# Earlier row loads, later filter weights and a third inverse-output buffer in a fused spectral filter and gated linear kernel

## The chip, the cores and the metric

The kernel runs on one core of a Trainium2 chip. The metric is the time of one execution on the device in microseconds (us). All runs that this text compares were classed as fast. Four of them had a granted clock of 0.992, the others 1.00: two timed runs of u2 and two of u8, one of these profiled. They are the slowest of their kernels; the medians and ratios include them, and the text on u2 and u8 says what is left without them.

Engines are named as in the profile: PE is TensorE's matmuls, PEld its weight loads, DVE is VectorE, ACT is ScalarE, SP is SyncE, which only issues transfers (SPq and ACTq lines are issues).

## The reference

```python
def _A_ref(x, w_r, w_i):                       # x: 1 x 2048 x 640, bf16
    X = rfft2(x.astype(f32), axes=(-2, -1))
    return irfft2(X * (w_r + 1j * w_i), s=(S, D), axes=(-2, -1)).astype(bf16)

def _B_ref(x, w_gate, w_up, w_down):           # 640 -> 1536 -> 640
    h = einsum("bsd,df->bsf", x, w_gate) * einsum("bsd,df->bsf", x, w_up)
    return einsum("bsf,fd->bsd", h, w_down)

xn = layernorm(x)                              # over the 640 columns
return x + _A_ref(xn, A_w_r, A_w_i) + _B_ref(xn, B_w_gate, B_w_up, B_w_down)
```

## The kernel before

The kernel is written as tasks (a load, a group of matmuls, a vector operation) with declared reads, writes, a priority and an **assumed duration**. A list scheduler in Python places them once, when the program is built. The result is one fixed order of instructions per engine; on the chip each engine runs its list and waits on semaphores. So a changed duration in the text does not change what is computed or how long it takes, but it can change every order after it.

The work has three stages for VectorE. First come normalisation of 16 row blocks, their transposes and the forward transform. Then come the products with the filter weights (D, C, WM below). Last come eight groups of inverse transforms (I, then V1 to V5 on VectorE), whose results (IV) are added to the down projection (ACC). Gate/up units (GU, ten matmuls each) fill PE beside the first two stages, accumulations beside the third.

```python
def dma(name, dst, src, nbytes, writes, prio, semkey=None, reads=(), after=(), q="sp"): ...
def copy_on(c, dst, src):                      # evict PSUM on ACT or on DVE
    ...
dma("ld_sm", V("SM"), ...)                     # small tables, 96 KB in one load, ACT's queue
# (cut)
for gi, (b0, nb) in enumerate(_X_LOADS):       # rows
    dma("ld_x%d" % gi, ..., prio=(0.0, 0.01, 0.02, 0.03, 0.042, 0.06)[gi])
# (cut) gate and up weights, five pieces each
    prio=(0.004, 0.012, 0.022, 0.032, 0.05)[i] + 0.001 * w_
# (cut) statistics of a row block, one task of two instructions on DVE
def em_bn(c, b=b):
    c.e.bn_stats(v_st[:, b, 0:6], v_x[:, b, 0:320])
    return c.e.bn_stats(v_st[:, b, 6:12], v_x[:, b, 320:640])
# (cut) transposes: blocks 0 to 3 on PE (T0), 4 to 15 by DMA (xt)
T("xt%d" % b, "sp", opts.get("xt_issue", 1500.0), em_xt, ...)
# (cut) filter weights, 64 rows each
dma("ld_w%d_%d_%d" % (t, w_, h), ..., prio=9.5 + 0.05 * t, after=[wpad])
# (cut) inverse transform of column group a, and its eviction into one of two buffers
ti = T("I_%d" % a, "pe", 5 * _d_mm(128), em_i, ...)
gr = (a // 2) % 2
ei = T("eI_%d" % a, ("act", "dve"), ..., writes=[(b_tc, ("r", 2 * gr + un, 2 * gr + un + 1))], frees=ti)
```

## Time and profile before

The median was 212.7 us (three runs, 212.59 to 213.03). The profiled run itself took 213.35 us, so its trace is about 0.5 us slower than a usual run; differences read between traces come out that much too large against the timed runs.

| us in the trace of before | |
|---|---|
| span | 211.5 |
| first gate/up matmul on PE | 8.16 |
| first product of the second stage | 88.1 |
| first inverse transform | 142.8 |
| last inverse group ends on VectorE | 199.3 |
| last matmul starts | 208.5 |

To read "how far ahead" one kernel is at a moment t, I sum the plain durations of all matmuls that have started by t (55.6 ns for 128 columns, 109.2 for 256, 135.9 for 320, the mean spacing of their starts where they run on) and subtract the same sum of before. The one under way counts up to t, and the dummy matmuls of the first 7 us are left out. This is called **PE's lead** here. PE does the same work in all these kernels (193.7 us in this count), so the lead at the end is the time gained.

### The profile page before, as it was taken

What the parts mean: (1) busy time and instruction counts of PE and PEld (TensorE: products, weight loads), DVE (VectorE), ACT (ScalarE), POOL (GpSimd) and SP (SyncE); (2) the same over time, 40 slices, a digit from 0 to 9 for tenths busy, and PEclk for the clock granted to TensorE, in tenths of its full rate; (3) what the DMA queues carried; (4) which work ended last, traced back from release to release, by engine and by line L of the source; (5) the groups of instructions that cost most, each with busy time, mean ns of one, the idle gap of its engine ahead of it and who ended that gap; (6) DMA issues with size and microseconds to landing.
All of it is one profiled execution on the core that took longest, in us unless ns stands there. A gap on an engine that the chain in (4) does not pass through costs nothing.

```text
span 211.5 us, 5204 instructions
## 1 busy us (share of the span) xinstructions
PE 202.6 (96%) x2044; PEld 169.4 (80%) x2044; DVE 185.1 (87%) x536; ACT 122.1 (58%) x281; POOL 0.2 (0%) x4
## 2 busy tenths in 40 slices
PE   8799999799999999989999999999999899999994
PEld 7699899688898998978888898898766677667773
DVE  3699989899999989389999999948999999999821
ACT  2375899799866666878999897776222202200000
POOL 0000000000000000000000000000000000000000
PEclk9999999999999999999999999999999999999999
DMA  6999999531133000002224233025042223222411
GB/s 190 304 341 395 384 299 218 104 62 31 34 64 65 0 3 0 0 18 56 56 58 120 55 62 90 3 62 155 3 121 82 64 63 108 81 77 65 126 47 47
DMA packets 30456, 21.74 MB, mean 103 GB/s; under 512 B 10336, under 2 KB 29408, under 8 KB 30304
## 3 DMA queue, kind: packets, MB, share of 16 engines
q1 hardware_dynamic: 28320, 20.34, 35.6%
q10 hardware_dynamic: 2112, 1.08, 1.9%
q8 instruction: 16, 0.26, 0.5%
q14 instruction: 8, 0.07, 0.1%
HBM read 16.82 MB, written 2.62 MB: 92 GB/s over the span
## 4 chain that ended last, share of the span: by engine, by line
PE 67%; DVE 22%; DMA 6%; issue 3%; ACT 1%; SPq 0%; DVEq 0%
PE ps L951 41%; PE ps L1172 12%; DMA arena<-arena 3%; DMA arena<-in_A_x_dram 2%; PE ps L1070 2%; PE ps L1071 2%; DVE arena L1187 2%; PE ps L994 2%; PE ps L912 2%; DVE arena L1144 1%; DVE arena L1145 1%; DVE arena L1153 1%; DVE arena L1137 1%; PE ps L1015 1%; ACT arena L709 1%
## 5 line engine op out<-in xcount | busy, mean ns | idle before, releaser
L709 ACT ACTIVATE arena<-ps 128x512 bf16<-128x512 f32 (+5 forms) x189 | 99.9, 572 | 55.0 <-PE ps L1099 28.2
L951 PE MATMUL ps<-arena 128*128 128x256 bf16 (+1 forms) x1080 | 112.8, 261 | 2.8 <-DMA arena<-arena 1.2
L951 PEld LDWEIGHTS ps<-arena 128*128 128x128 bf16 x1080 | 93.6, 98 | 14.2 <-ACT arena L709 1.6
L1172 PE MATMUL ps<-arena 128*128 128x320 bf16 x384 | 56.5, 299 | 0.3 <-DVE arena L1187 0.3
L1172 PEld LDWEIGHTS ps<-arena 128*128 128x128 bf16 x384 | 37.2, 98 | 14.7 <-DVE arena L1187 0.7
L966 DVE TENSOR_TENSOR arena<-arena 128x512 bf16<-128x512 bf16 (+1 forms) x54 | 21.1, 390 | 10.5 <-ACT arena L709 10.4
L1030 DVE TENSOR_TENSOR arena<-ps,arena 128x256 f32<-128x256 f32 x64 | 22.6, 414 | 0.0
L1187 DVE TENSOR_TENSOR arena<-ps,arena 128x320 bf16<-128x320 f32 x32 | 15.4, 482 | 6.7 <-PE ps L1180 6.7
L1071 PE MATMUL ps<-arena 128*128 128x128 bf16 x80 | 10.7, 219 | 0.0
L1070 PE MATMUL ps<-arena 128*128 128x128 bf16 x80 | 10.6, 219 | 0.0
L1180 PE MATMUL ps<-arena 128*128 128x320 bf16 x32 | 9.1, 300 | 0.5 <-DVE arena L1154 0.4
L1070 PEld LDWEIGHTS ps<-arena 128*128 128x128 bf16 x80 | 8.7, 112 | 0.5
L865 DVE TENSOR_TENSOR arena<-arena 128x384 f32<-128x384 bf16 x16 | 8.8, 550 | 0.0
L1071 PEld LDWEIGHTS ps<-arena 128*128 128x128 bf16 x80 | 8.7, 112 | 0.1
L769 DVE BATCH_NORM_STATS2 arena<-arena 128x6 f32<-128x320 bf16 x8 | 3.9, 489 | 3.8 <-DMA arena<-in_A_x_dram 3.7
L1033 DVE TENSOR_TENSOR arena<-ps,arena 128x260 f32<-128x260 f32 x16 | 7.1, 441 | 0.0
L1045 DVE TENSOR_TENSOR arena<-arena 128x256 bf16<-128x256 f32 x16 | 6.7, 421 | 0.2
L1054 ACT ACTIVATE arena<-arena 128x256 bf16<-128x256 bf16 x16 | 6.6, 414 | 0.3 <-DVE arena L1049 0.2
L1049 DVE TENSOR_TENSOR arena<-arena 128x256 bf16<-128x256 f32 x16 | 6.7, 418 | 0.0
L866 DVE TENSOR_TENSOR arena<-arena 128x256 f32<-128x256 bf16 x16 | 6.7, 417 | 0.0
L1152 DVE TENSOR_TENSOR arena<-arena 128x640 bf16<-128x640 f32 x8 | 6.5, 818 | 0.1
L762 ACT ACTIVATE arena<-arena 128x640 bf16<-128x640 bf16 x8 | 6.6, 828 | 0.0
(71 smaller groups left out, 212.2 us busy)
## 6 DMA issues: line engine op xcount, KB each, us to landing
arena<-in_A_x_dram SPq DMA_DIRECT2D x20, 160.0 KB, 2.6
out_dram<-arena SPq DMA_DIRECT2D x32, 80.0 KB, 1.6
arena<-c_tf SPq DMA_DIRECT2D x4, 384.0 KB, 11.8
arena<-in_A_w_r_dram SPq DMA_DIRECT2D x32, 40.1 KB, 2.4
arena<-in_A_w_i_dram SPq DMA_DIRECT2D x32, 40.1 KB, 2.2
arena<-in_B_w_gate_dram SPq DMA_DIRECT2D x4, 320.0 KB, 7.9
arena<-in_A_x_dram SPq DMA_DIRECT2D x1, 1280.0 KB, 12.1
arena<-c_ti SPq DMA_DIRECT2D x2, 512.0 KB, 14.5
```

Source lines behind the costliest of these rows:

```text
L709: return c.e.activation(dst, src, _ACTF.Copy)
L865: c.e.tensor_tensor(uo[:, o, :, 0:3, :], v_xb[:, b:b + 2, 0:6:2, :], v_xb[:, b:b + 2, 5:10:2, :], op)
L866: ins = c.e.tensor_tensor(uo[:, o, :, 3:5, :], v_xb[:, b:b + 2, 6:10:2, :], v_xb[:, b:b + 2, 1:5:2, :], op)
L951: ins = c.e.matmul(ps[:, bk, w * n:(w + 1) * n], v_gw[:, w, j, ft, :], v_xt[:, j, rows], start=(j == 0), stop=(j == 4))
L966: return c.e.tensor_tensor(v_ht[:, ft0:ft0 + 2, rows], v_gbf[:, rr, :, 0:n], v_gbf[:, rr, :, n:2 * n], _OP.mult)
L1030: c.e.tensor_tensor(v_p[:, r2, w, :, 128 * h:128 * h + 128].rearrange("p c (m k) -> p c m k", k=4), xh.rearrange("p c (m k) -> p c m k", k ...
L1033: ins = c.e.tensor_tensor(v_p[:, r2, :, :, 256:321], ps[:, bk:bk + 2, 256:321].unsqueeze(1).to_broadcast([128, 2, 2, 65]), v_w[:, wr, :, 0 ...
L1070: c.e.matmul(dst, l1, v_ti[:, t, 0, :], start=True, stop=False)
L1071: ins = c.e.matmul(dst, l2, v_ti[:, t, 1, :], start=False, stop=True)
L1172: ins = c.e.matmul(ps[:, bk, 0:320], v_ht[:, ft, a * 128:(a + 1) * 128], v_wd[:, ft, sl3], start=(ft == 7), stop=False)
L1180: return c.e.matmul(ps[:, bank_of(ag2), 0:320], v_sm[:, 2, :], v_v[:, a, sl3], start=False, stop=True)
L1187: return c.e.tensor_tensor(v_out[:, a % 2, sl3], ps[:, bk, 0:320], v_xr[:, xs, sl3], _OP.add)
```

## The change

It has four parts. The **head** part loads row block 1 ahead of the gate weights, cuts the small table in two (32 KB now, 64 KB later) and splits the statistics of a row block into two tasks, those of block 1 tied behind block 0's work. The **weights** part ties filter weights, inverse tables and down weights behind the last normalisation, so that the row transposes are not issued behind them. The **third** part adds a third buffer for inverse outputs, in the memory of the gate/up staging buffer. The **constants** part corrects assumed durations and the affinity (how unwilling the scheduler is to put an eviction on the second of its two engines).

```diff
-_DMA_LAT = 1000.0
-_DMA_ISSUE = 440.0
+_DMA_LAT = 1300.0
+_DMA_ISSUE = 520.0
... (ACT +25 ns, DVE +7 and +12 ns, each normalisation step 15 to 80 ns more; cut)
+        b_tc3 = alloc("TC3", 2560, at=lay["GBF"][0])
-        dma("ld_sm", V("SM"), d_sm.rearrange("p t n -> p (t n)"), 128 * 768, [(b_sm, None)], prio=0.002, q="act")
+        dma("ld_sm0", v_sm[:, 0, :], d_sm[:, 0, :], 128 * 256, [(b_sm, ("t", 0, 1))], prio=0.002, q="act")
+        dma("ld_sm1", v_sm[:, 1:3, :], d_sm[:, 1:3, :], 128 * 512, [(b_sm, ("t", 1, 3))], prio=0.25)
... (the readers of the table wait for their part only; cut)
-                [(b_x, ("s", b0, b0 + nb))], prio=(0.0, 0.01, 0.02, 0.03, 0.042, 0.06)[gi])
+                [(b_x, ("s", b0, b0 + nb))], prio=(0.0, 0.003, 0.02, 0.03, 0.042, 0.06)[gi])
+                    for i in range(2):
+                        ... bn_stats of half i, a task of its own (cut)
+                    if b == 1:
+                        bns[0].deps.add(muls[0])
+                        bns[1].deps.add(e0_first)
-                    T("xt%d" % b, "sp", opts.get("xt_issue", 1500.0), em_xt, ...
+                    T("xt%d" % b, "sp", opts.get("xt_issue", 1100.0), em_xt, ...
-                gu = T("GU_%d_%d" % (ft, b0), "pe", 10 * _d_mm(n), em_gu,
+                gu = T("GU_%d_%d" % (ft, b0), "pe", 10.15 * _d_mm(n), em_gu,
-                        semkey=("w", wr), after=[wpad])
+                        semkey=("w", wr), after=[wpad, muls[opts.get("w_after", 15)]])
... (the same "after" on the inverse tables and down weights; cut)
+            gt = (a // 2) % 3
+            bt, k0 = (b_tc, 2 * gt) if gt < 2 else (b_tc3, 0)
-        sch.affinity = opts.get("affinity", 600.0)
+        sch.affinity = opts.get("affinity", 1500.0)
```

More of the change, by code (lines that the diff above doesn't have):

```diff
@@ L517, in _d_dve @@
 def _d_dve(n):
-    return n * 1.04 + 65.0
+    return n * 1.04 + 72.0
 def _d_dve_psum(n):
-    return n * 1.04 + 70.0
+    return n * 1.04 + 82.0
 def _d_dve_psum16(n):
@@ L537, in _d_act @@
 def _d_act(n):
-    return n * 0.833 + 80.0
+    return n * 0.833 + 105.0
 class _Ctx(object):
@@ L656, in _build @@
         v_y = V("Y").rearrange("p (r n) -> p r n", r=2)
-        v_tc = V("TC").bitcast(_F32).rearrange("p (r s u n) -> p r s u n", r=2, s=5, u=2)
+        v_tc2 = V("TC").bitcast(_F32).rearrange("p (r s u n) -> p r s u n", r=2, s=5, u=2)
+        v_tc = [v_tc2[:, 0], v_tc2[:, 1], V("TC3").bitcast(_F32).rearrange("p (s u n) -> p s u n", s=5, u=2)]
         v_vt = V("VT").bitcast(_F32).rearrange("p (r s q b) -> p r s q b", r=2, s=4, q=4)
@@ L767, in _build, with em_bn @@
                 else:
-                    def em_bn(c, b=b):
-                        c.e.bn_stats(v_st[:, b, 0:6], v_x[:, b, 0:320])
-                        return c.e.bn_stats(v_st[:, b, 6:12], v_x[:, b, 320:640])
-                    T("bn%d" % b, "dve", 800.0, em_bn, reads=[(b_x, ("s", b, b + 1))],
-                      writes=[(b_st, ("b", b, b + 1))], prio=pbase)
+                    bns = []
+                    for i in range(2):
+                        def em_bn(c, b=b, i=i):
+                            return c.e.bn_stats(v_st[:, b, 6 * i:6 * i + 6], v_x[:, b, 320 * i:320 * i + 320])
+                        bns.append(T("bn%d_%d" % (b, i), "dve", 420.0, em_bn, reads=[(b_x, ("s", b, b + 1))],
+                                     writes=[(b_st, ("b", 2 * b + i, 2 * b + i + 1))], prio=pbase))
+                    if b == 1:
+                        bns[0].deps.add(muls[0])
+                        bns[1].deps.add(e0_first)
                     def em_ag(c, b=b):
                         return c.e.bn_aggr(v_mv[:, b, :], v_st[:, b, :])
-                    T("ag%d" % b, "dve", 130.0, em_ag, reads=[(b_st, ("b", b, b + 1))],
+                    T("ag%d" % b, "dve", 176.0, em_ag, reads=[(b_st, ("b", 2 * b, 2 * b + 2))],
                       writes=[(b_mv, ("b", b, b + 1))], prio=pbase)
@@ L781, in em_mb @@
                     return c.e.tensor_scalar(v_mv[:, sl_, 1], v_ss[:, sl_], 1.0 / _D, None, _OP.mult)
-                T("mb%d" % b0, "dve", 160.0, em_mb, reads=[(b_m32, ("b", b0, b0 + nb)), (b_ss, ("b", b0, b0 + nb))],
+                T("mb%d" % b0, "dve", 211.0, em_mb, reads=[(b_m32, ("b", b0, b0 + nb)), (b_ss, ("b", b0, b0 + nb))],
                   writes=[(b_mv, ("b", b0, b0 + nb))], prio=pbase)
@@ L788, in em_ve @@
                 return c.e.tensor_scalar(v_ve[:, sl_], v_mv[:, sl_, 1], 1e-5, None, _OP.add)
-            T("ve_%d" % gi, "dve", 80.0, em_ve, reads=[(b_mv, gk)], writes=[(b_ve, gk)], prio=pbase - 0.006)
+            T("ve_%d" % gi, "dve", 95.0, em_ve, reads=[(b_mv, gk)], writes=[(b_ve, gk)], prio=pbase - 0.006)
             def em_sd(c, sl_=sl_):
                 return c.e.activation(v_sd[:, sl_], v_ve[:, sl_], _ACTF.Sqrt)
-            T("sd_%d" % gi, "act", 120.0, em_sd, reads=[(b_ve, gk)], writes=[(b_sd, gk)], prio=pbase - 0.006)
+            T("sd_%d" % gi, "act", 200.0, em_sd, reads=[(b_ve, gk)], writes=[(b_sd, gk)], prio=pbase - 0.006)
             def em_rs(c, sl_=sl_):
                 return c.e.reciprocal(v_rs[:, sl_], v_sd[:, sl_])
-            T("rs_%d" % gi, "dve", 80.0, em_rs, reads=[(b_sd, gk)], writes=[(b_rs, gk)], prio=pbase)
+            T("rs_%d" % gi, "dve", 126.0, em_rs, reads=[(b_sd, gk)], writes=[(b_rs, gk)], prio=pbase)
             for b in range(b0, b0 + nb):
@@ L803, in em_sub @@
                     return c.e.tensor_scalar(v_x[:, b, :], v_x[:, b, :], v_mv[:, b, 0:1], None, _OP.subtract)
-                T("sub%d" % b, "dve", 290.0, em_sub, reads=[(b_mv, ("b", b, b + 1))],
+                T("sub%d" % b, "dve", 305.0, em_sub, reads=[(b_mv, ("b", b, b + 1))],
                   writes=[(b_x, ("s", b, b + 1))], prio=pb - 0.005)
@@ L810, in em_mul @@
                     return c.e.tensor_scalar(v_x[:, b, :], v_x[:, b, :], v_rs[:, b:b + 1], None, _OP.mult)
-                muls[b] = T("mul%d" % b, ("dve", "act") if b >= 4 else "dve", {"dve": 290.0, "act": _d_act(640) + 93}, em_mul, reads=[(b_rs, ("b", b, b + 1))],
+                muls[b] = T("mul%d" % b, ("dve", "act") if b >= 4 else "dve", {"dve": 310.0, "act": _d_act(640) + 93}, em_mul, reads=[(b_rs, ("b", b, b + 1))],
                   writes=[(b_x, ("s", b, b + 1))], prio=pb)
@@ L816, in em_xt @@
                         return c.e.dma_start_transpose(v_xt[:, :, b * 128:(b + 1) * 128], v_x[:, b, :])
-                    T("xt%d" % b, "sp", opts.get("xt_issue", 1500.0), em_xt, reads=[(b_x, ("s", b, b + 1))],
+                    T("xt%d" % b, "sp", opts.get("xt_issue", 1100.0), em_xt, reads=[(b_x, ("s", b, b + 1))],
                       writes=[(b_xta, ("s", b * 128, (b + 1) * 128)), (b_xtb, ("s", b * 128, (b + 1) * 128))], prio=pb, nbytes=128 * 1280)
@@ L830, in em_t0 @@
                     return ins
-                t0 = T("T0_%d" % b, "pe", 5 * _d_mm(128), em_t0, reads=[(b_x, ("s", b, b + 1)), (b_sm, None)],
+                t0 = T("T0_%d" % b, "pe", 5 * _d_mm(128), em_t0, reads=[(b_x, ("s", b, b + 1)), (b_sm, ("t", 0, 1))],
                        prio=pb, bank="pair" if b < opts.get("e0_split", 2) else "single", cls="a")
@@ L844, in _build @@
                     hold(t0, es_)
+                    if b == 0:
+                        e0_first = es_
                     continue
@@ L915, in _build @@
                 tr = T("R_%d" % (b + u), "pe", 5 * _d_mm(128), em_r,
-                       reads=[(b_f, ("r", 3 * gr, 3 * gr + 3)), (b_sm, None)], prio=pf, bank="pair", cls="a")
+                       reads=[(b_f, ("r", 3 * gr, 3 * gr + 3)), (b_sm, ("t", 1, 3))], prio=pf, bank="pair", cls="a")
                 def em_er(c, b=b + u, tr=tr):
@@ L974, in _build @@
             dma("ld_ti%d" % q, v_ti[:, 8 * q:8 * q + 8], d_ti[:, 8 * q:8 * q + 8], 128 * 8 * 512,
-                [(b_wd, ("e", 2048 * q, 2048 * q + 2048))], prio=9.0 + 0.3 * q)
+                [(b_wd, ("e", 2048 * q, 2048 * q + 2048))], prio=9.0 + 0.3 * q, after=[muls[opts.get("w_after", 15)]])
         for t in range(16):
@@ L1086, in _build @@
             dma("ld_wd%d" % f0, v_wd[:, f0:f1], wdv[:, f0:f1], 128 * (f1 - f0) * 1280,
-                [(b_wd, ("e", 640 * f0, 640 * f1))], prio=18.0 if f0 < 7 else 9.6)
+                [(b_wd, ("e", 640 * f0, 640 * f1))], prio=18.0 if f0 < 7 else 9.6, after=[muls[opts.get("w_after", 15)]])
         for a in range(16):
@@ L1104, in _build, with em_ei @@
             gr = (a // 2) % 2
+            gt = (a // 2) % 3
             un = a % 2
-            def em_ei(c, ti=ti, gr=gr, un=un):
+            bt, k0 = (b_tc, 2 * gt) if gt < 2 else (b_tc3, 0)
+            def em_ei(c, ti=ti, gt=gt, un=un):
                 bk = bank_of(ti)
-                return copy_on(c, v_tc[:, gr, :, un, :],
+                return copy_on(c, v_tc[gt][:, :, un, :],
                                psflat[:, bk * 512: bk * 512 + 640].rearrange("p (s n) -> p s n", s=5))
             ei = T("eI_%d" % a, ("act", "dve"), {"dve": _d_dve_psum(640), "act": _d_act(640)}, em_ei,
-                   writes=[(b_tc, ("r", 2 * gr + un, 2 * gr + un + 1))], prio=pa - 0.001, frees=ti)
+                   writes=[(bt, ("r", k0 + un, k0 + un + 1))], prio=pa - 0.001, frees=ti)
             hold(ti, ei)
@@ L1116, in _build, with em_v1 @@
             b_ = a - 1
-            def em_v1(c, gr=gr):
-                b1r, b1i, b2r, b2i = [v_tc[:, gr, i].rearrange("p u n -> p (u n)") for i in range(4)]
+            def em_v1(c, gr=gr, gt=gt):
+                b1r, b1i, b2r, b2i = [v_tc[gt][:, i].rearrange("p u n -> p (u n)") for i in range(4)]
                 vt = v_vt[:, gr].rearrange("p s q b -> p s (q b)")
@@ L1124, in em_v1, with em_v2 @@
                 return c.e.scalar_tensor_tensor(vt[:, 3], b1i, _RT, b2i, _OP.mult, _OP.subtract)
-            T("V1_%d" % b_, "dve", 4 * _d_dve(256), em_v1, reads=[(b_tc, ("r", 2 * gr, 2 * gr + 2))],
+            T("V1_%d" % b_, "dve", 4 * _d_dve(256), em_v1, reads=[(bt, ("r", k0, k0 + 2))],
               writes=[(b_vt, ("r", gr, gr + 1))], prio=pa - 0.001)
-            def em_v2(c, gr=gr):
-                a_ = v_tc[:, gr, 4].rearrange("p u (o b) -> p (u o) b", o=2)
+            def em_v2(c, gr=gr, gt=gt):
+                a_ = v_tc[gt][:, 4].rearrange("p u (o b) -> p (u o) b", o=2)
                 c.e.scalar_tensor_tensor(v_vy[:, gr], v_vt[:, gr, 0], -0.25, a_, _OP.mult, _OP.add)
@@ L1132, in _build @@
             T("V2_%d" % b_, "dve", 2 * _d_dve(256), em_v2,
-              reads=[(b_vt, ("r", gr, gr + 1)), (b_tc, ("r", 2 * gr, 2 * gr + 2))],
+              reads=[(b_vt, ("r", gr, gr + 1)), (bt, ("r", k0, k0 + 2))],
               writes=[(b_vy, ("r", gr, gr + 1)), (b_ve2, ("r", 2 * gr, 2 * gr + 1))], prio=pa - 0.001)
@@ L1182, in _build @@
                 iv = T("IV_%d_%d" % (a, hf), "pe", _d_mm(320), em_iv,
-                       reads=[(b_v, ("a", a, a + 1)), (b_sm, None)], prio=pc + 0.01 + 0.001 * hf - 22.0, after=[ag2])
+                       reads=[(b_v, ("a", a, a + 1)), (b_sm, ("t", 1, 3))], prio=pc + 0.01 + 0.001 * hf - 22.0, after=[ag2])
                 def em_f1(c, ag2=ag2, a=a, xs=xs, sl3=sl3):
```

## The prediction

> **What bounds the kernel now.** I read the page first: the busy shares, then the span in 40 slices.
>
> ```profile
> PE 202.6 (96%) x2044; PEld 169.4 (80%) x2044; DVE 185.1 (87%) x536; ACT 122.1 (58%) x281; POOL 0.2 (0%) x4
> ...
> PE   8799999799999999989999999999999899999994
> ...
> DVE  3699989899999989389999999948999999999821
> ```
>
> TensorE (PE) looks full, but VectorE (DVE) is full too: its row is nines from about 10 to 90 us, 95 to 142 and 148 to 195, with weak slices only at the start, around 92, around 145, and at the end. The program has three DVE stages, and PE fills its time beside them with gate/up matmuls (line 951), later with down-projection matmuls (line 1172). The table by stage says it in numbers:
>
> ```profile
> core 0: us, PE busy (x) PEld busy (x) DVE busy (x) ACT busy (x) POOL busy (x), PEclk, DMA share, GB/s
> 10.00:88.00 78.00, 76.56 (x837) 68.02 (x835) 72.20 (x220) 61.18 (x134) 0.00 (x0) 1.00 0.52 138
> ...
> 95.00:142.00 47.00, 47.00 (x523) 41.68 (x522) 43.99 (x146) 40.71 (x109) 0.00 (x0) 1.00 0.27 64
> ...
> 151.00:165.00 14.00, 13.17 (x107) 9.20 (x105) 13.96 (x35) 2.60 (x4) 0.00 (x0) 1.00 0.26 77
> 165.00:199.00 34.00, 33.11 (x259) 23.73 (x258) 33.93 (x83) 3.90 (x6) 0.00 (x0) 1.00 0.30 88
> 199.00:209.00 10.00, 9.84 (x73) 6.80 (x70) 3.25 (x9) 0.00 (x0) 0.00 (x0) 1.00 0.17 51
> ```
>
> From 151 to 199 DVE is busy 47.89 of 48 us; its last inverse group (line 1154) ends at 199.3, one group every 7.0 us. PE takes 7.7 us for what belongs to a group (four half-row accumulations at 1.77 us, two inverses at 0.28), so it falls behind: it waits for a group until 164.4 and never after, and when DVE is done PE still has five accumulations, 9 us, of which four could have been open earlier. So two chains run side by side: DVE sets when the inverse groups come up to 165, PE's fixed work sets the end from there. The whole possible gain is PE's idle time, next read from the waits and, more finely, from matmul start to start: after the first real matmul (8.16 us) I count 6.7 us in 22 gaps. The largest are 1.37 (at 37.6), 0.75 (91.6), 0.58 (157.4), 0.46 (160.0), 0.30 (164.4), 0.59 (166.6), 0.29 (180.7) and 0.51 us (188.6). The head before 8.16 is the other loss.
>
> The head, in the timeline:
>
> ```profile
> 6.36 0.38 ACT L709 ACTIVATE arena<-ps 128x256 bf16<-128x256 bf16 x1 [1.24 <-PE ps L828]
> 6.87 0.49 DVE L769 BATCH_NORM_STATS2 arena<-arena 128x6 f32<-128x320 bf16 x1 [1.14 <-DMA arena<-in_A_x_dram]
> 7.68 0.34 DVE L710 COPY arena<-ps 128x384 bf16<-128x384 bf16 x1
> 8.16 1.28 PE L951 MATMUL ps<-arena 128*128 128x128 bf16 x20 [0.95 <-DVE arena L775]
> 9.71 3.54 PEld L951 LDWEIGHTS ps<-arena 128*128 128x128 bf16 x60 [0.17 <-DMA arena<-in_B_w_gate_dram]
> 10.40 0.49 DVE L769 BATCH_NORM_STATS2 arena<-arena 128x6 f32<-128x320 bf16 x1
> ```
>
> ScalarE (ACT) evicts its half of row block 0's transpose at 6.36. DVE's half could go then too, but stands in program order behind the statistics of row block 1, which wait for their data until 6.87; it runs at 7.68. The second wait, at 9.71, is for gate weights.
>
> The middle, in the chain that ended last:
>
> ```profile
> 32.16 6.45 DMA arena<-arena
> 38.61 0.46 issue
> 39.07 1.27 PE ps L951 x10
> ```
>
> The first DMA transpose (row block 4) is issued only at 32.16 and lands at 38.61; PE stands 1.37 us. Block 4's last normalisation step had ended at 25.7. SyncE (SP) was issuing tables and filter weights between: 16 filter-weight loads of 0.6 to 2.3 us, two table loads and one of down weights, from 17.3 to 32.1.
>
> The tail, in the waits of PE:
>
> ```profile
> PE ps L951 <- DMA arena<-arena: 1.2, 1, 1.2
> ...
> PE ps L1099 <- DVE arena L1131: 0.7, 2, 0.4
> ...
> PE ps L1180 <- DVE arena L1154: 0.4, 1, 0.4
> ```
>
> Line 1099 is the inverse transform; 1131 is the last reader of its output buffer (two slots). Line 1180 waits for a finished inverse group, whose last instruction is 1154.
>
> **What the Trainium skill says.** (1) "PSUM — Partial Sum Buffer", section "Engine vs sequencer instructions": ScalarE's and VectorE's queues are strict FIFO, and matmuls run in program order. The trace agrees: the eviction above stood 1.3 us (6.36 to 7.68) behind an instruction that waited for data. (2) "DMA: Bandwidth & Descriptors", section "Issuing engines are not separate DMA queues": loads from SyncE and ScalarE run on the same 16 engines and interleave. The trace agrees: the pieces of gate weights (SP) and up weights (ACT) land interleaved, 5.33 and 6.28, then 9.67 and 8.40 us, and from 3.5 to 14.2 us the eight pieces of 320 KB and three row blocks of 160 KB come at some 290 GB/s. So moving one load forward pushes others back by its bytes. (3) "Perfetto Trace Analysis", section "Optimization Strategy", says that a kernel can have several regimes whose most-contended engine changes; the stage table agrees.
>
> **The change part by part.**
>
> *Row block 1 before gate weights; its statistics split.* SP issues x0, x1, gate; the 96 KB small table becomes 32 KB now and 64 KB later. x1 landed at 6.85; about 164 KB behind x0 (3.54) with up weights sharing the engines, an estimate of 4.5. Gate piece 0 lands later by x1's bytes less the table's: (160 - 64) KB / 290 GB/s = 0.3 us on the 6.28 at which both first pieces were there, so 6.6. One half of the statistics is tied behind the normalisation of block 0 (ends 5.74) and the other behind the first eviction. The eviction then runs at about 6.36 and ends at 6.7; the first gate/up matmul starts at about 6.85 instead of 8.16: 1.3 us. But I do not book 1.3. Those 20 matmuls last 1.2 us, to 8.1. What comes next needs either gate piece 1, which landed at 9.67 and has nearly the same bytes ahead of it (9.4 to 9.6), or block 1's transpose. From the start of its aggregation to the end of its eviction took 7.93 to 10.12, 2.2 us; with aggregation at 7.1 it is ready at 9.3. So continuous PE work starts at about 9.4 instead of 9.71: **0.3 us**. For DVE, block 2's statistics at 10.40 come right on its landing at 10.38; the order ahead of it is unchanged, so DVE gains about 0.2 from the smaller table and 0.3 from work moved into its idle time: **0.4 to 0.5**.
>
> *Filter weights behind the row transposes.* The transpose of block 4 can issue at about 25.8 and lands, at 2.7 us typical (the page's median), or some 2 us more behind the tables still in flight until 29, by 31. PE needs it at 37.3. The **1.37 us** gap goes. DVE waits 0.91 us at 41.3 for gate/up results that this gap delayed; that goes too. The filter weights are first needed near 91 (line 1030 at 91.21); the last normalisation ends at 66.5 and the last transpose is issued by 68, and 23 us remain for what took 15 us to issue: no new wait.
>
> *Third buffer of inverse outputs.* It shares memory with the gate/up staging buffer, so its first fill waits for the last product (146.96 in the profile, ends 147.4): harmless, as these inverses ran at 153.7. The inverse waits at 160.0, 166.6 and 180.7, 1.33 us together, can go. But from 152 to 165 PE is limited by DVE: it has at most four accumulations open and waits for line 1154 at 157.4 and 164.4. Time freed before 164.4 only lengthens these waits. What counts is after 164.4: the 0.59, the 0.29, and one pair of inverses (10 matmuls of 0.056 us, 0.56) done before instead of after. Of these 1.4 us I book **0.9**.
>
> *Other constants.* Durations and the choice between ACT and DVE (600 to 1500) only reorder. Only 5 of some 194 evictions and copies of lines 709/710 are on DVE, four of them matter little; a normalisation of 0.38 us may move from ACT to DVE. I book 0, with about 1 us either way for the new order.
>
> *Sum.* PE is ahead by 0.3 + 1.37 = 1.7 us at 40 us. DVE is ahead by 0.45 + 0.91 = 1.35, and DVE decides when the three stages change. So 1.35 counts up to the tail, plus 0.9, plus an allowance of 0.7 for the smaller ACT and DVE waits between 28 and 94 us (DVE's largest are 2.35 at 85.5 and 0.85 at 88.3), which better durations may shorten. Together 2.95, rounded up to 3.1 because the new settings look tuned as a set: 212.7 - 3.1 = **209.6 us**.
>
> **Rivals.** (a) *DVE keeps everything*: PE's earlier work only turns into longer waits at 157 and 164, DVE does not move, and just the tail is gained: about 211.8. For it: DVE full from 151 to 199. Against: its 0.91 us wait at 41.3 hangs directly on the late transpose. (b) *The head counts in full*: 1.3 instead of 0.3, all inverse waits (1.33) and half of the 0.75 at 91.6 go: 1.3 + 1.37 + 1.33 + 0.4 is 4.4, plus reordering, 207.5 to 208.3. For it: these are all real PE gaps. Against: gate piece 1 cannot land earlier, and DVE limits 152 to 165. (c) *A worse order*: the stage borders (85 to 94, 139 to 144, where DVE already idles some 8 us) are placed by a static schedule; an extra gate/up pair, 2.2 us, ahead of the critical step would eat most of the gain: 211.5 to 212.5.
>
> **Range and chances.** (a) to (c) span 207.5 to 212.5; eight in ten lie within 207.7 to 211.9. Two per cent is 208.4, reached only if the head or a stage border gives more than I book: 0.24. A slowdown over 2% would need several misplacements together: 0.02.
>
> **What would show it.** Right: the first line 951 matmul near 6.9, then a new PE idle of about a microsecond near 8.1 to 9.3; first row transpose issued near 26 and no wait on it; no wait of line 1099 on 1131; DVE's last line 1154 some 1 to 2 us before 198.9; still over 95% PE. Wrong: continuous PE from 7 us on (gain up to 1 us more); a wait of line 1030 on filter weights near 90; or waits of line 1180 near 157 and 164 longer by just what was gained before.

## The result

The changed kernel took 210.79 us (median of 4 runs, 210.61 to 211.21), the kernel before on the same chip 212.87 (212.59 to 213.29). The ratio is 0.9904, 95% interval 0.988 to 0.9927: 1% faster, "same" at a limit of 2%. A ratio is the mean time of one kernel's fast runs over that of the other's of the same rounds, so it is not quite the ratio of the medians.

The page of the changed kernel, busy shares and slices:

```profile
PE 201.7 (96%) x2044; PEld 170.5 (82%) x2044; DVE 184.3 (88%) x536; ACT 122.3 (59%) x281; POOL 0.2 (0%) x4
...
PE   7789999999999999989999999999999999999994
...
DVE  4599999999999999389999999965999999999941
```

The shares are those of before; a gain of 2 us cannot be seen in them. The slices differ at the start, where PE's first three are 7, 7 and 8 (8, 7 and 9 before).

The stage table, with the windows that the prediction showed (same columns):

```profile
10.00:88.00 78.00, 77.14 (x858) 69.51 (x856) 72.39 (x220) 61.53 (x135) 0.00 (x0) 1.00 0.51 139
95.00:142.00 47.00, 47.00 (x515) 41.69 (x513) 42.95 (x143) 41.30 (x108) 0.00 (x0) 1.00 0.26 62
151.00:165.00 14.00, 14.00 (x116) 10.25 (x115) 13.97 (x35) 2.60 (x4) 0.00 (x0) 1.00 0.28 78
165.00:199.00 34.00, 33.67 (x260) 24.25 (x258) 33.97 (x82) 2.60 (x4) 0.00 (x0) 1.00 0.31 90
199.00:209.00 10.00, 7.37 (x55) 5.09 (x52) 2.87 (x7) 0.00 (x0) 0.00 (x0) 1.00 0.16 49
```

From 151 to 199 PE is busy 47.67 us where it was 46.28, and DVE is as full as it was. After 199 PE has 7.37 us of work left instead of 9.84: this is the gain. DVE's last inverse group ends at 199.10, only 0.2 us earlier than before, so VectorE did not become faster; PE fell less far behind it.

The head, in the timeline:

```profile
6.07 0.36 DVE L712 COPY arena<-ps 128x384 bf16<-128x384 bf16 x1
...
7.38 1.12 PEld L960 LDWEIGHTS ps<-arena 128*128 128x128 bf16 x20 [0.74 <-DMA arena<-in_B_w_gate_dram]
7.38 1.29 PE L960 MATMUL ps<-arena 128*128 128x128 bf16 x20 [0.57 <-DVE arena L795]
...
8.86 0.39 DVE L817 TENSOR_SCALAR arena<-arena 128x640 bf16<-128x640 bf16 x1
...
9.66 1.29 PE L960 MATMUL ps<-arena 128*128 128x128 bf16 x20 [0.98 <-DMA arena<-in_B_w_gate_dram]
...
10.55 0.89 DVE L774 BATCH_NORM_STATS2 arena<-arena 128x6 f32<-128x320 bf16 x2 [1.10 <-DMA arena<-in_A_x_dram]
...
10.78 0.44 PE L835 MATMUL ps<-arena 128*128 128x128 bf16 x5
...
11.36 0.34 DVE L712 COPY arena<-ps 128x384 bf16<-128x384 bf16 x1
...
11.84 2.48 PE L960 MATMUL ps<-arena 128*128 128x128 bf16 x40 [0.61 <-DVE arena L782]
```

Block 0's eviction now runs at 6.07 (7.68 before), and the first gate/up matmuls start at 7.38, when gate piece 0 has landed (at 7.34; 5.33 before). The weight load (PEld) names this wait; the line of PE names DVE, whose work for this pair had ended at 6.43. They end at about 8.5, and PE stands until gate piece 1 lands at 9.61. The last normalisation step of block 1 (line 817) ended at 9.25, but its transpose (line 835) stands in PE's order behind this second pair and runs at 10.78, where before it ran ahead of the second pair, at 9.28. So PE stands again until 11.84, while ACT (until 11.64) and DVE (11.36 to 11.70) evict it. On DVE this eviction stands behind the statistics of block 2, which waited for their rows until 10.55; that costs little here, since the transpose's own matmuls last until 11.22.

The waits of PE (engine and line, what it waited for, us in total, times, longest):

```profile
PE ps L960 <- DMA arena<-in_B_w_gate_dram: 1.0, 1, 1.0
PE ps L960 <- DVE arena L782: 0.6, 1, 0.6
...
PE ps L1108 <- DVE arena L1142: 0.3, 1, 0.3
PE ps L921 <- DMA arena<-c_sm: 0.2, 1, 0.2
```

The wait for a transpose (arena from arena, 1.2 us) is gone; SP issues the first one at 27.74 instead of 32.16, and it lands at 32.89. The inverse (now line 1108) waits once for the last reader of its output buffer, 0.3 us instead of twice 0.7 in all; the wait for a finished inverse group (0.4) is gone. New is the last line: the forward transform (line 921) waits for the second half of the small table. From matmul start to matmul start that costs 0.42 us, and the chain that ended last now runs through this load:

```profile
13.37 10.82 DMA arena<-c_sm
```

SP issued it at 13.37, behind the last, 1280 KB row load, and it landed at 24.19.

PE's lead over before, in us of matmul work:

| t | 12 | 25 | 37.5 | 40 | 54 | 90 | 140 | 157 | 166 | 190 | 205 |
|---|---|---|---|---|---|---|---|---|---|---|---|
| changed | -0.90 | -1.21 | -1.11 | +0.25 | +1.02 | +1.02 | +0.80 | +0.38 | +1.65 | +2.47 | +2.47 |

So PE is *behind* by about 1 us through the first 37 us, gets 1.36 back at the old transpose wait, 0.77 between 40 and 54, and 1.67 after 140. The lead at the end, 2.47, answers to the spans' 2.4 us. In the tail PE's stands sum to 2.7 us in before and 1.0 in the changed kernel. Gone are, among them, the two for a finished inverse group, 0.58 us at 157.5 and 0.30 at 164.6.

### The profile page after: what moved, and what is told of

It is laid out like the page before. It is cut to its first block, busy times and chain, and to the rows that moved or that the text cites. A ratio compares the mean times of both kernels' runs of the same rounds, so it can differ in the third digit from the quotient of the medians.

```text
span 209.1 us, 5208 instructions
## 1 busy us (share of the span) xinstructions
PE 201.7 (96%) x2044; PEld 170.5 (82%) x2044; DVE 184.3 (88%) x536; ACT 122.3 (59%) x281; POOL 0.2 (0%) x4
## 3 DMA queue, kind: packets, MB, share of 16 engines
q10 hardware_dynamic: 2112, 1.02, 1.9%
## 4 chain that ended last, share of the span: by engine, by line
PE 77%; DVE 9%; SPq 6%; DMA 5%; issue 2%; ACT 1%; DVEq 0%
PE ps L960 44%; PE ps L1183 17%; SPq L705 6%; DMA arena<-c_sm 5%; PE ps L921 2%; PE ps L1080 2%; PE ps L1079 2%; PE ps L1003 2%; PE ps L1191 1%; PE ps L1108 1%; PE ps L1024 1%; PE ps L1027 1%; PE ps L1026 1%; PE ps L1025 1%; DVE arena L1198 1%
## 5 line engine op out<-in xcount | busy, mean ns | idle before, releaser
L774 DVE BATCH_NORM_STATS2 arena<-arena 128x6 f32<-128x320 bf16 x16 | 7.2, 478 | 3.4 <-DMA arena<-in_A_x_dram 3.2
L1003 PE MATMUL ps<-arena 128*128 128x128 bf16 (+1 forms) x80 | 6.6, 219 | 0.0
```

The lines of the kernel that those rows point to most:

```text
L1003: ins = c.e.matmul(psflat[:, bk * 512 + k * 128: bk * 512 + k * 128 + n], v_uq[:, k, t, :], v_fd[:, k * 128: k * 128 + n], start=True, sto ...
```

## The experiments

Twelve kernels were run, all correct, with five rounds each. The kernel before took 212.85 (first four), 213.01 (next four), 212.96 (next three) and 213.08 us (last) in the same rounds.

| label | what it is | median us | ratio to before, 95% |
|---|---|---|---|
| (changed) | all four parts | 210.79 | 0.9904, 0.988 to 0.9927 |
| u1_no_head | changed, head part undone | 213.6 | 1.004, 1.0025 to 1.0055 |
| u2_no_weights | changed, weights part undone | 211.37 | 0.9942, 0.9919 to 0.9964 |
| u3_no_third | changed, third buffer undone | 211.67 | 0.9946, 0.9933 to 0.996 |
| u4_no_consts | changed, constants undone | 212.94 | 1.0008, 0.9996 to 1.002 |
| u5_only_weights | before plus weights part | 212.4 | 0.9974, 0.996 to 0.9988 |
| u11_only_head | before plus head part | 212.83 | 0.999, 0.9977 to 1.0002 |
| u12_only_consts | before plus constants | 214.7 | 1.0075, 1.006 to 1.0089 |
| u6_head_order | changed, block 1 moved in the orders | 210.72 | 0.9898, 0.9881 to 0.9914 |
| u7_table_early | changed, second small-table half earlier | 211.03 | 0.9913, 0.9898 to 0.9928 |
| u8_x2_early | changed, row block 2 before gate piece 1 | 211.83 | 0.994, 0.9914 to 0.9965 |
| u9_x1_behind | changed, row block 1 behind gate piece 0 | 210.94 | 0.9902, 0.9887 to 0.9917 |
| u10_head_gates | u6 and u7 together, and one ACT move | 209.96 | 0.9855, 0.9841 to 0.9868 |

My theory was the prediction's own account: each part removes a wait of its own, and the waits add up. The main rival was that the parts work through the order that the scheduler makes of them, so that a part's value depends on the others.

### One part undone

**u1_no_head**

```diff
-        dma("ld_sm0", ...); dma("ld_sm1", ...)
+        dma("ld_sm", V("SM"), ..., q="act")
-                    prio=(0.0, 0.003, 0.02, ...)
+                    prio=(0.0, 0.01, 0.02, ...)
... statistics of a block again one task
```

> The changed kernel without its first part (row block 1 before the gate weights, small table split, statistics split); everything else kept. Ledger theory (from comparing how much matmul work is done at each moment in the two traces): the first part costs PE 0.8 us by 14 us and another 0.35 us by 24 us (wait for the second half of the small table), so without it PE is up to 1.1 us further ahead and the time is 209.7 to 210.3. Rival A (the prediction's step): the part is worth +0.3 us, so 211.1. Rival B: VectorE carries the middle, PE's loss in the head does not matter, 210.6 to 211.0.

It took 213.6 us, slower than before, and outside every expectation. In the head PE's lead at 12 us is -0.5, better than the changed kernel's -0.90, and there is no small-table wait. (It is still a loss against before: in this plan too block 1's transpose stands behind the second gate/up pair.) But the new plan holds 81 gate/up units ahead of the first product of the second stage instead of 77. That product starts at 90.76 (87.09 in the changed kernel) for four units of 1.09 us, and the first inverse transform at 145.12 (142.00). Four more units done early leave four fewer to run beside the end of the second stage. The window from 142 to 151 in this kernel, then in the changed one:

```profile
142.00:151.00 9.00, 7.36 (x82) 5.54 (x80) 5.09 (x15) 7.53 (x15) 0.00 (x0) 1.00 0.44 129
```

```profile
142.00:151.00 9.00, 8.76 (x93) 7.22 (x92) 7.10 (x17) 6.56 (x11) 0.00 (x0) 1.00 0.32 93
```

PE (first figure) idles 1.64 us there, and DVE (third) loses 2. PE's lead falls from +1.5 at 140 to -1.0 at 150. So this run does not measure the head part; it measures where the stage border fell when the plan was made anew.

**u2_no_weights**

```diff
-                        semkey=("w", wr), after=[wpad, muls[opts.get("w_after", 15)]])
+                        semkey=("w", wr), after=[wpad])
... the same for inverse tables and down weights
```

> The changed kernel with the filter weights again ahead of the row transposes; the orders on PE, VectorE and ScalarE are identical to the changed kernel, only SyncE's order moves. Ledger theory: the wait for row block 4's transpose comes back with about 1.4 us and is not absorbed: 211.9 to 212.3. Rival: VectorE decides up to 165 us, so most is absorbed there: 210.8 to 211.3.

It took 211.37 us (211.03 to 212.53): 0.6 more than the changed kernel, between the two expectations. But the two slowest runs (212.24 and 212.53) are those with a clock of 0.992; the other four have a median of 211.16, 0.4 more than the changed kernel and within the rival's range. The orders of PE, DVE and ACT are those of the changed kernel; only SP's differs. The first transpose is issued at 31.95, as late as before, yet PE's gap there is 0.46 us from start to start, not 1.37. PE comes to this point about 1 us later than in before (lead -0.97 at 37.5, -0.06 at 40), because the head had cost it that much. So the rest of the wait was not absorbed by VectorE later: it did not arise. A late transpose hides a late head, and the reverse.

**u3_no_third**

```diff
-            gt = (a // 2) % 3
-            bt, k0 = (b_tc, 2 * gt) if gt < 2 else (b_tc3, 0)
+            gt = gr
+            bt, k0 = b_tc, 2 * gt
```

> The changed kernel with two instead of three buffers of inverse outputs. Ledger theory: the tail (after 150 us) gave 1.7 us of PE's lead, all by this buffer: 212.3 to 212.8, with waits of the inverse on line 1142's equivalent back (three of 0.3 to 0.6 us). Prediction's step: 0.9 us, so 211.7. Rival: the tail's waits went because VectorE was ahead, not because of the buffer: 210.8 to 211.2.

It took 211.67 us, 0.9 more than the changed kernel, as the prediction's step said. The wait for the inverse buffer is back in PE's timeline of this kernel:

```profile
167.32 0.72 PE L1106 MATMUL ps<-arena 128*128 128x128 bf16 x10 [0.17 <-DVE arena L1138]
174.06 0.72 PE L1106 MATMUL ps<-arena 128*128 128x128 bf16 x10 [0.43 <-DVE arena L1138]
```

PE's lead still grows by 0.9 us in the tail (0.77 at 140, 1.71 at 205), against 1.67 in the changed kernel. So the third buffer is not the only thing that helps there.

**u4_no_consts**

```diff
-_DMA_LAT = 1300.0
-_DMA_ISSUE = 520.0
+_DMA_LAT = 1000.0
+_DMA_ISSUE = 440.0
... all durations and the affinity as before; the other three parts stay
```

> The changed kernel with the old durations and the old preference between ScalarE and VectorE; only the static order changes. Ledger theory: PE's lead grew by 0.7 us between 42 and 54 us because waits on ScalarE's evictions went; if the new durations did that, 211.3 to 211.6, with 0.2 to 0.3 us waits of gate/up matmuls on ScalarE back at 44 to 53 us. Rival: the transposes landing early did it, and the constants are worth nothing: 210.5 to 211.0.

It took 212.94 us, the time of before; both expectations were too small. PE's lead is +0.59 at 54 us, +0.50 at 140 and +0.44 at 205: with old constants the third buffer gives nothing in the tail. The timeline of PE shows how:

```profile
153.10 0.72 PE L1108 MATMUL ps<-arena 128*128 128x128 bf16 x10 [0.29 <-DVE arena L1142]
...
159.85 0.72 PE L1108 MATMUL ps<-arena 128*128 128x128 bf16 x10 [0.43 <-DVE arena L1142]
```

With its shorter durations for DVE, the scheduler pulls inverses 8 to 11 forward to places that DVE has not reached on the chip. PE waits for the buffer again, 0.46 and 0.59 us from start to start, and the accumulations behind wait with it. In the changed kernel's order the same inverses stand one accumulation later and do not wait.

### One part alone

**u5_only_weights** (the weights edit above, in the kernel before)

> The kernel before with nothing but the filter weights behind the row transposes; orders on PE, VectorE and ScalarE as before, only SyncE's order moves. The prediction's step: the 1.37 us wait for row block 4 goes, VectorE's 0.91 us wait at 41 goes, 0.9 to 1.4 us come through: 211.4 to 211.9. Rival: it is absorbed where PE waits for VectorE at 157 and 164, as most of it was when this part was undone alone: 212.3 to 212.8.

It took 212.4 us, 0.6 less than before. The number is that of the rival, in which VectorE keeps most of it; the trace is not. Orders on PE, DVE and ACT are those of before. PE's lead goes from +0.23 at 37.5 to +1.60 at 40, the whole 1.37, and +1.19 remain at the end. PE's stands for a finished group are as long as in before (0.59 us at 156.3 and 0.30 at 163.4), and all eight inverse groups on DVE end 1.2 us earlier (the first at 149.84, 151.04 before, the last at 198.15, 199.34 before). The spans differ by 1.1 us (211.5 and 210.4) and the timed medians by 0.6. Here the profiled run of before is 0.34 above its median and that of this kernel 0.23 below, which accounts for the rest. So the wait is removed in full, and 0.6 us of it by the timed runs, 1.1 to 1.2 by this pair of traces, reaches the end.

**u11_only_head** (the head edit, in the kernel before)

> The kernel before with the first part of the change alone, old durations. Theory: PE loses about 0.8 us by 14 us (second pair waits for gate piece 1 with row block 1's transpose behind it) and some more at the small table; nothing gives it back: 212.8 to 213.6. The prediction's step (+0.3 to 0.45 us): 212.4 to 212.7.

It took 212.83 us, 0.1 less than before, with an interval that includes none. PE's lead is -1.06 at 12 and -0.88 at 37.5, so the head is worse for PE here too. It turns to +0.19 at 40, since PE comes late to the late transpose and waits less for it (0.30 us instead of 1.37). The head's loss is hidden under the old wait.

**u12_only_consts** (the constants edit, in the kernel before)

> The kernel before with only the scheduler's new durations and affinity. Undoing them in the changed kernel cost 2.1 us. If they are worth that on their own, by a better order, this kernel takes 210.6 to 211.3 us. My theory says that they pay only together with the third buffer, and that what decides is where the planner puts the border of the second stage: its printed order has 81 gate/up units before the first D product here, as in the kernel without the head part, and 77 in the kernels before and after. Four units of 1.09 us that come early are no loss by themselves, but VectorE enters the second stage later and PE has none of them left at 143 us. So I expect slower than before: 213.4 to 214.8 us, the first D product some 3 to 4 us later than in before (88.1), and PE idle by more than 1 us between 142 and 148.

It took 214.7 us, 1.6 more than before. The plan has 81 units ahead of the second stage, its first product starts at 91.20 (88.11 in before), and PE idles 2.3 us of the window from 142 to 151:

```profile
142.00:151.00 9.00, 6.71 (x76) 5.12 (x74) 5.09 (x15) 6.41 (x13) 0.00 (x0) 1.00 0.45 129
```

PE's lead falls from +1.07 at 140 to -1.90 at 150. Two plans with 81 units were run, this one and u1, and both lose over 2 us at this place; no plan with 77 does. (The counts are also those of the traces: 810 gate/up matmuls ahead of the first product here and in u1, 770 in all others.) Without any edit of the head, PE's lead at 12 us is -0.78 here. Undoing the constants costs 2.1 us and adding them alone costs 1.6: they have no value of their own.

### The head

The next five keep the changed kernel's planned orders as they are and move single tasks in them; `move(engine, task, before)` puts a task ahead of another, and the waits are computed again.

**u6_head_order**

```diff
+        sch.move("pe", "T0_1", "GU_2_0")             # block 1's transpose after one gate/up pair, not two
+        sch.move("act", "sd_1", "eG_0_0")            # block 1's root ahead of the first gate/up eviction
+        sch.move("act", "eT0_1_act", "eG_1_0")
+        sch.move("dve", "eT0_1_dve", "bn2_0")        # its eviction ahead of block 2's statistics
```

> The changed kernel with its planned order kept everywhere but in the head: row block 1's transpose ahead of the second pair of gate/up matmuls on PE, its square root ahead of the first eviction on ScalarE, its eviction ahead of row block 2's statistics on VectorE. PE's stands at 8.6 (1.15 us) and 11.15 (0.78 us) shrink to one of about 1 us: PE gains 0.7 to 1.0 us by 14 us, VectorE next to nothing (it waits for row block 2, 10.5). If PE's lead decides: 209.8 to 210.1. If VectorE's chain decides up to 165 us: 210.5 to 210.9.

It took 210.72 us, no better than the changed kernel. The moves work: PE's lead is 0.0 at 20 us instead of -0.78. But at 25 it is -1.06. PE came early to the forward transform and waited for the small table, in the timeline of PE:

```profile
24.09 0.73 PE L958 MATMUL ps<-arena 128*128 128x128 bf16 x10 [0.89 <-DMA arena<-c_sm]
```

**u7_table_early**

```diff
+        sch.move("sp", "ld_sm1", "ld_x5")            # ahead of the last, 1280 KB row load
```

> The changed kernel with the second half of the small table issued ahead of the last row load, everything else in the planned order. The 0.42 us PE wait at 23.9 goes. If PE's lead decides: 210.3 to 210.5. If VectorE's chain decides: 210.6 to 210.9.

It took 211.03 us, again no gain. The forward transform no longer waits (23.49), and the lead at 25 is -0.45. But at 28 it is -1.36. In the timeline ACT stands in front of the statistics of row block 8 for its rows, with gate/up evictions behind them, and PE stands for those:

```profile
24.12 0.74 ACT L796 ACTIVATE arena<-arena 128x640 bf16<-128x640 bf16 x1 [0.93 <-DMA arena<-in_A_x_dram]
...
27.17 1.05 PE L997 MATMUL ps<-arena 128*128 128x256 bf16 x8 [0.77 <-ACT arena L748]
```

**u8_x2_early**

```diff
+        sch.move("sp", "ld_x2", "ld_gw2_0")          # row block 2 ahead of gate piece 1
```

> The changed kernel with row block 2 loaded ahead of the second gate piece, everything else in the planned order. Row block 2 lands near 9.2 instead of 10.5, gate piece 1 near 10.2 instead of 9.6: VectorE's chain starts up to 1.1 us earlier, PE loses 0.5 us at the second pair. If VectorE's chain decides: 209.7 to 210.2. If PE's lead decides: 211.1 to 211.4.

It took 211.83 us, worse than the changed kernel. The two slowest of its six runs (212.52 both) have a clock of 0.992; the other four have a median of 211.47 (210.83 to 211.86). So the expectation by VectorE's chain failed, and that by PE's lead came near. Gate piece 1 lands at 10.5 us, and in PE's timeline the first hole is 2.3 us long instead of 1.15:

```profile
7.08 1.29 PE L997 MATMUL ps<-arena 128*128 128x128 bf16 x20 [0.22 <-DMA arena<-in_B_w_gate_dram]
10.54 2.06 PE L997 MATMUL ps<-arena 128*128 128x128 bf16 x20 [2.16 <-DMA arena<-in_B_w_gate_dram]
```

PE's lead is -1.5 at 12 us. What follows is not read: the profile is one of the two at 0.992, its granted clock is 0.50 from 11 to 14 us, and its matmuls start at twice the usual spacing there.

**u9_x1_behind**

```diff
+        sch.move("sp", "ld_x1", "ld_gw2_0")          # row block 1 behind gate piece 0, as before the change
```

> The changed kernel with one load moved back: row block 1 behind the first gate piece, as before; the planned order of every engine is kept. It separates the load from the re-planning that came with undoing the whole first part. Theory now: the load itself moves little, because the second pair of gate/up matmuls waits for gate piece 1 (9.6) and VectorE for row block 2 (10.5) either way: 210.6 to 211.2. Rival: the load is what undoing the first part cost (2.8 us): 212 or more. The first pair should start at 7.4 to 7.8 (VectorE's half of the first statistics now stands ahead of the first eviction and waits for row block 1, near 6.5 to 6.9).

It took 210.94 us, which is not told apart from the changed kernel. Gate piece 0 lands at 5.36 and row block 1 at 6.86, as before the change; with row block 1 first these are 7.34 and 4.19. PE's lead at 12 us is -0.78 and -0.90. So the row load, the first thing that the title names, is worth 0.1 us or nothing in this order: the first pair needs a gate and an up piece, the later of which lands at 7.29 here and at 7.34 there (up last here, gate last there), and starts at 7.79 and 7.38. The second pair waits for gate piece 1 in both (9.56 here, 9.61 there).

**u10_head_gates**

```diff
+        ... the four moves of u6 and the move of u7
+        sch.move("act", "sm8", "eG_10_0")            # block 8's statistics behind four gate/up evictions
```

> The changed kernel with three repairs in its planned order: the head order of the sixth run, the small table early as in the seventh, and ScalarE's statistics of row block 8 (which wait for the last row load, 24.0) behind the four evictions that stood behind them. Theory: each of the two repairs alone was swallowed by the next thing that waits for a late load, at 23.3 (table) or 26.3 (ScalarE behind row block 8); with all three, PE and VectorE are both about 0.9 us ahead of the changed kernel from 28 us on, and it lasts to the end: 209.7 to 210.1. Rival: another wait takes their place again, 210.5 to 211.

It took 209.96 us (209.88 to 210.0), 3.0 less than before and some 0.8 less than the changed kernel: it beats both. PE's lead is +0.05 at 12 us, +0.04 at 25, +1.92 at 54 and +3.37 at 205. The head in its timeline of PE:

```profile
9.06 0.45 PE L872 MATMUL ps<-arena 128*128 128x128 bf16 x5 [0.32 <-DVE arena L854]
9.45 2.23 PEld L997 LDWEIGHTS ps<-arena 128*128 128x128 bf16 x40
9.45 2.41 PE L997 MATMUL ps<-arena 128*128 128x128 bf16 x40
```

From 9.45, just after gate piece 1 landed (9.40), PE runs 40 matmuls without a wait; in the changed kernel it has 20 of them and a hole there. Three gates stood one behind the other. The first two gave nothing one at a time (u6, u7), all three together 0.8 us; the third was not mended alone.

## Why the prediction was right, and where its steps were not

The class and the range were right: 210.79 us within 207.7 to 211.9. The steps booked 3.1 us and 2.1 came. That the sum came so near is in part luck: the head lost what it was to gain, and the tail gave almost twice what was booked. Against the changed kernel's lead:

| step | booked us | measured |
|---|---|---|
| head | +0.3 PE, +0.45 DVE | -1.2 PE at 25 us; DVE none (block 2's statistics at 10.55, 10.40 before) |
| transposes | 1.37 PE, 0.91 DVE | +1.36 PE (37.5 to 40); DVE's wait at 41 is gone |
| allowance for smaller waits, 28 to 94 us | 0.7 | +0.77 (40 to 54) |
| other constants | 0, about 1 either way | see the text |
| third buffer | 0.9 | 0.9 us (u3) |
| up to the tail, all together | 2.05 | +0.80 at 140 us |
| tail, all together | 0.9 | +1.67 (140 to 205) |

**Head: wrong in sign.** The step that failed is the sentence "So continuous PE work starts at about 9.4 instead of 9.71". I had block 1's transpose ready at 9.3, and its rows were (9.25); but in the new plan the transpose stands behind the second gate/up pair on PE and runs at 10.78, so after the wait for gate piece 1 there is a second hole, to 11.84. This hole is not the head part's alone: u12 and u1, which lack that part, have it too (11.01 to 11.72 and 10.76 to 11.47). In all kernels planned anew the transpose stands behind the second pair; in before and in u5, with the order of before, it does not. I had also written that "the order ahead of it is unchanged" of block 2's statistics on DVE; it was not, block 1's eviction now comes after them.

Two sizes were off as well. The first matmul starts at 7.38, not 6.9: both first pieces were there at 7.34 and not at 6.6, 1.06 us later than the 6.28 of before where I had taken bytes over bandwidth, 0.3. That alone would have cost little: in u9 the first pair starts later still (7.79), and the time is the same. And the split of the table, which I booked as a gain, cost 0.42 us at its second half. u6, u7 and u10 show that these are gates of order and of late loads, and what repairing them gives: the lead at 25 us rises from -1.21 to +0.04.

**Transposes: right in mechanism**, and in size on PE's lead; in time, u5 alone gave 0.6 us. The first transpose was issued at 27.74, not 25.8, and landed at 32.89, not by 31, and PE still did not wait for it. u5 has the part alone, 1.37 us of lead. u2 costs less only because a late PE waits less.

**DVE decides up to the tail: not shown, and not needed.** I let 1.35 of PE's 1.7 count because DVE sets the stage changes. PE had lost the head instead; +0.25 at 40 us came to +0.80 at 140 us. DVE ended its last group 0.2 us earlier, not 1 to 2. The end was set by PE's fixed work, as the prediction also said of the time after 165.

**Allowance: right in sum.** It came from 42 to 54 us, where PE's gaps behind evictions on ACT shrank; u4 has some of these back (0.19, 0.10 and 0.28 us from 43 to 46) and gains only 0.07 from 40 to 54, so the better durations did it.

**Third buffer: right in size, wrong in what it needs.** Undoing it costs 0.9. But u4 has the buffer and no gain in the tail. And the step "Time freed before 164.4 only lengthens these waits" failed: the two waits for a finished group, 0.88 us together, are gone. PE runs inverses 8 and 9 at 153.9 where before ran 6 and 7, and comes to the two places at 157.71 and 165.41, when DVE's groups had ended, at 157.27 and 164.29.

**Other constants: mis-sized.** I booked 0, and undoing them costs 2.1. They are not worth 2.1 either, since alone they cost 1.6 (u12). What they do is a plan: together with the third buffer they give a tail order in which one inverse waits (0.49 us at 173.9) and not three (1.32 us together in before; lead +1.67 in the tail, +0.9 without the buffer, -0.1 without the constants). Together with the head part they keep the stage border at 77 units; without it they give 81.

Of the rivals, (a), 211.8, fell: the waits at 157 and 164 are gone in the changed kernel, and in u5, where they stay, the transpose gain did not lengthen them. (b), 207.5 to 208.3, fell with the head. (c), an extra gate/up pair ahead of the critical step, did not happen in the changed kernel, but it did in u1 and u12, with two pairs.

The costs of undoing are 2.8, 0.6 (0.4 at the full clock), 0.9 and 2.1 us, over 6 together, and the gain is 2.1. The parts do not add. What remains open is the value of the head part under a fixed plan: u1 mixes it with the stage border. It is open too whether u10 needs its third move. And why the scheduler packs 81 units in two of the plans was not traced to one duration.

## What to carry to other kernels

Where a program is ordered by a planner with assumed durations, undo a part both by planning anew and by moving one task in the frozen plan; only the second leaves the rest of the plan as it was. When a wait is removed at the head of a kernel, list all the waits that would follow within the time gained (here gate piece 1, an eviction, a table, a row load) before booking anything, and remove them together. And a loss upstream of a fixed arrival costs nothing until that arrival is mended, so the order of repairs changes what each seems to be worth.

## What the Trainium skill lacked or had wrong

- "DMA: Bandwidth & Descriptors", section "Issuing engines are not separate DMA queues", says that loads from several engines share the 16 engines and interleave, which these runs confirm. It gives no size for it: with a 160 KB row load issued ahead of it on SP, gate piece 0 landed at 7.34 us instead of 5.36 (the changed kernel and u9), 2.0 us for bytes that take an estimated 0.55 at the 290 GB/s seen there. Up piece 0, issued by ACT, landed at 5.33 instead of 7.29, so the later of the two hardly moved, and gate piece 1 stayed at 9.6.
- "PSUM — Partial Sum Buffer", section "Engine vs sequencer instructions", states strict FIFO queues for ScalarE and VectorE. The traces agree, and the section gives no price for it in a planned program: in before DVE's half of block 0's eviction stood 1.3 us, 6.36 to 7.68, behind statistics that waited for rows, and one statistic behind a late load on ACT cost PE 0.94 us from start to start (u7, 26.23 to 27.17).
- "Perfetto Trace Analysis", section "Optimization Strategy", advises to find the gaps on the contended engine and what blocks each. It lacks that gaps mended singly can give nothing: u6 and u7 gave 0.1 and -0.2 us, and together with one more move 0.8.
